# Folding packed attention values into the first expert weight: full-array fp32r products through DRAM, or fp32 products in 64x32 tiles kept on chip

## The chip, the cores and the metric

The kernel runs on one core of a Trainium2 chip. The metric is the device time of one execution in microseconds (us). The kernel before took 1387.21 us, the median of three runs (1386.0 to 1388.96). The engines of the core are called as in the profile: PE (matrix products, with PEld for its weight loads), DVE and POOL (elementwise work), ACT (activations, copies and casts), and SP, which here only issues DMAs.

## The reference

Two attentions follow one another, then a mixture of four experts that all run on every token:

```
p_packed = softmax(p k^T / 8) v            # 32 packed rows for each batch and head
out      = softmax(q p_packed^T / 8) p_packed
x        = out, heads side by side         # (8*576, 512)
y        = sum over e of  prob[:, e] * (relu(x @ w1[e]) @ w2[e])
```

There are 8 batches, 8 heads, 576 tokens per batch, head size 64; w1 is 4 x 512 x 1024 and w2 is 4 x 1024 x 512. Inputs and output are fp32.

## The kernel before

**No x is ever formed.** The second attention's weights (called xh and xl, their rounded high part and the remainder) are kept transposed: 8 heads x 32 packed rows = 256 rows, in two groups `g` of 128. Since x @ w1 = weights @ (p_packed @ w1), the kernel folds p_packed into w1 first: G = p_packed @ w1, 256 rows for each batch, formed per chunk of 512 columns of one expert's w1. There are 8 such chunks (`NCH`), two for each expert.

**Precision.** Matrix products run in fp32r, each operand split in a high part (a cast, line 86, `hi_of`) and a low part (source minus high part, line 91, `lo_of`), three products for each pair. Scores, transposes and the product with v run as plain fp32 matmuls. The profile lists each plain fp32 matmul as two records, except transposes.

**The main loop** goes over 64 units: 4 pairs of batches (`sb`), for each 8 chunks (`ch`), for each the two batches of the pair. A unit is `even` for the first batch of the pair and `odd` for the second. A unit makes:
- `mm1_group` (L316): relu(G^T x) times the probability of the expert, four groups of 12 matmuls, evicted at L322 by DVE; it runs one unit ahead.
- `s_operand` (L339 sums on DVE, then a cast on ACT and a subtraction on POOL into `st`), two products ahead.
- `product` (L395): seven Strassen-like products with combinations of w2's blocks (`tt`), 12 matmuls each; the result is added to an accumulator by DVE (L405), copied for chunk 0 (L403), finished and stored for chunk 7 (L414).

So a unit has 84 matmuls of L395 and 48 of L316, all of 288 columns. PE executes its stream in order. The order in which the code issues work is a priority; a planner that simulates times places the instructions of each engine.

**Combinations of w2** are formed in the first pair of batches only, in the odd units (`t_form`, subtractions at L377 on POOL, casts on ACT and low parts on POOL), stored to DRAM from the even units (`t_store`) and loaded again for the later pairs (`t_load`).

**G before** takes four steps. (1) `w1_split` loads a chunk of w1, splits it and writes for each head a stack of 64 rows of high part and 64 rows of low part to DRAM (`wd`); `w1_first` does this for chunk 0 without the load back. (2) `w1_loaded` loads one head's stack (`w1st`). (3) `g_heads` multiplies it with the packed values of four batches at once (`pga`, `pgb`, made by six small POOL operations at L178 to L180): two matmuls of 512 columns over the full array per head, L263 and L266, a copy by ACT to `graw` (L270), and a DMA to DRAM (`gd`) issued by ACT. (4) `g_load` loads, for each unit, the two groups of its batch (`gk`, 128 rows x 512), which are split again into `ghl`, by ACT and by DVE in the first pair of batches, by ACT and POOL after it. `g_heads` runs for batches 0 to 3 ahead of the loop and in the first pair, for batches 4 to 7 in the units from the end of the second pair through the third.

**Attention parts.** `pack_unit(b, g)` does four heads of the first attention: scores (L129), maximum, exponential, normalisation, transposes (L150, L154), product with v (L162), copy to `ppbd` (L169), and the parts for `pga` and `pgb`. `tok_unit(b, g)` does the second attention's weights for four heads: scores (L196), transposes and softmax on DVE, high and low parts. Eight pack units (batches 0 to 3) and four tok units run ahead of the loop; the other eight pack units run in the second pair of batches, the other tok units at chunks 5 to 7.

The PSUM pools are `ps_aux`, two tiles of one bank, used by transposes, the product with v and G, and `ps_dbl`, three tiles of two banks. The tiles `kt`, `vt`, `at`, `a1` of the pool `att` have one buffer each and serve pack units, tok units and `t_form` in turn.

Of the kernel before, what the change touches and what calls it, by code (L numbers as in the profile page):

```python
# [23 lines left out]
HALF = B // 2  # L24
# [15 lines left out]
def attention_moe(ctx: ExitStack, tc: tile.TileContext, q, k, v, p, dp, w1, w2, out):  # L40
# [31 lines left out]
    nc.vector.tensor_copy(  # L72
        out=pgb.rearrange("p a h n b -> p (a h n b)").rearrange("p (c n) -> p c n", c=4),
        in_=ppbd[0].rearrange("p a n -> p (a n)").rearrange("p (c n) -> p c n", c=1).broadcast_to([P, 4, NPAIR * 2 * NPK]),
    )
# [3 lines left out]
    gd = [[dram.tile([H * NPK, HALF, FC], F32, name=f"gd{hf}_{c}") for c in range(NCH)] for hf in range(2)]  # L79
    td = [[dram.tile([P, 2 * 2 * DH], F32, name=f"td{c}_{i}") for i in range(NPROD)] for c in range(NCH)]  # L80
    wd = [[dram.tile([P, FC], F32, name=f"wd{c}_{h}") for h in range(H)] for c in range(NCH)]
    pnd = dram.tile([E, NTOK], F32, name="pnd")

# [21 lines left out]
    def pack_unit(b, g, new):  # L105
        bl = b % HALF
# [18 lines left out]
        )  # L125
        sps = dbl()
# [41 lines left out]
        for hh in range(2):  # L168
            nc.vector.tensor_copy(  # L169
                out=ppbd[bl][hh * D:(hh + 1) * D, prs, hh * NPK:(hh + 1) * NPK],  # L170
                in_=psv[hh * D:(hh + 1) * D],
            )
        yield
        for hh in range(2):
            rows, other = slice(hh * D, (hh + 1) * D), slice((1 - hh) * D, (2 - hh) * D)
            src = ppbd[bl][rows, prs, hh * NPK:(hh + 1) * NPK]
            hi = pga[rows, prs, hh, :, bl]
            nc.gpsimd.tensor_copy(out=hi, in_=src)  # L178
            lo_of(pgb[rows, prs, hh, :, bl], src, hi, nc.gpsimd)
            nc.gpsimd.tensor_copy(out=pga[other, prs, hh, :, bl], in_=hi)  # L180
# [4 lines left out]
    def tok_unit(b, g):  # L185
# [3 lines left out]
        qt = att.tile([P, 2, S], F32, name="kt")  # L189
        nc.sync.dma_start(out=qt, in_=q[b][:, 2 * g:2 * g + 2, :])  # L190
        a2 = att.tile([P, S // 32, NPK], F32, name="a1")
        a2f = a2.rearrange("p a n -> p (a n)")
        ps = dbl()
        for c in range(2):
            for j in range(2):
                nc.tensor.matmul(  # L196
                    out=ps[j * 64:(j + 1) * 64, c, 0:HS], lhsT=ppbd[b % HALF][:, 2 * g + j, :],
                    rhs=qt[:, j, c * HS:(c + 1) * HS], start=True, stop=True,
                )
# [14 lines left out]
        a2t = att.tile([P, S], F32, name="at")  # L214
# [5 lines left out]
    def w1_raw(ch, pr, tile_of):  # L220
        e, hf = divmod(ch, F // FC)
        raw = tile_of()
        nc.sync.dma_start(out=raw, in_=w1[e, pr * P:(pr + 1) * P, hf * FC:(hf + 1) * FC])
        return raw

    def w1_split(ch):

        for pr in range(NPAIR):
            raw = w1_raw(ch, pr, lambda: wpool.tile([P, FC], F32, name="wraw", bufs=2))
            whl = wpool.tile([P, 2, FC], F32R, name="whl")  # L230
            hi_of(whl[:, 0, :], raw, nc.scalar)
            lo_of(whl[:, 1, :], raw, whl[:, 0, :], nc.vector)
            yield
            for hh in range(2):
                rows, other = slice(hh * D, (hh + 1) * D), slice((1 - hh) * D, (2 - hh) * D)
                dst = wd[ch][2 * pr + hh]
                nc.sync.dma_start(out=dst[rows, :], in_=whl[rows, 0, :].bitcast(F32))
                nc.sync.dma_start(out=dst[other, :], in_=whl[rows, 1, :].bitcast(F32))
            yield

    def w1_first(raws):
        for pr, raw in enumerate(raws):
            for hh in range(2):
                rows, other = slice(hh * D, (hh + 1) * D), slice((1 - hh) * D, (2 - hh) * D)
                wst = wpool.tile([P, FC], F32R, name="w1st", bufs=3)
                hi_of(wst[rows, :], raw[rows, :], nc.scalar)
                nc.vector.tensor_tensor(
                    out=wst[other, :], in0=raw[rows, :], in1=wst[rows, :].bitcast(F32), op=ALU.subtract
                )
                nc.sync.dma_start(out=wd[0][2 * pr + hh], in_=wst.bitcast(F32))  # L250
                yield wst

    def w1_loaded(ch):
        for h in range(H):
            wst = wpool.tile([P, FC], F32R, name="w1st", bufs=3)
            nc.sync.dma_start(out=wst.bitcast(F32), in_=wd[ch][h])
            yield wst

    def g_heads(half, ch, tiles):
        for h, wst in enumerate(tiles):  # L260
            yield
            ps = aux()
            nc.tensor.matmul(  # L263
                out=ps, lhsT=pga[:, h // 2, h % 2].rearrange("p n b -> p (n b)"), rhs=wst, start=True, stop=False
            )
            nc.tensor.matmul(  # L266
                out=ps, lhsT=pgb[:, h // 2, h % 2].rearrange("p n b -> p (n b)"), rhs=wst, start=False, stop=True
            )
            graw = gpool.tile([P, FC], F32, name="graw", bufs=2)
            nc.scalar.copy(out=graw, in_=ps)  # L270
            nc.scalar.dma_start(
                out=gd[half][ch][h * NPK:(h + 1) * NPK].rearrange("n b f -> (n b) f"), in_=graw
            )
            yield

    units = [(sb, ch, 2 * sb + i) for sb in range(SB) for ch in range(NCH) for i in range(2)]
    gs = {}

    def g_load(u):
        sb, ch, b = units[u]  # L280
        gs[u] = []
        for g in range(NG):
            gk = gpool.tile([P, FC], F32, name="gk", bufs=2)
            bl = b % HALF
            nc.sync.dma_start(
                out=gk,
                in_=gd[b // HALF][ch][g * P:(g + 1) * P, bl, :],
            )
            ghl = gpool.tile([P, 2, FC], F32R, name="ghl", bufs=4)
            hi_of(ghl[:, 0, :], gk, nc.scalar)  # L290
            lo_of(ghl[:, 1, :], gk, ghl[:, 0, :], nc.vector if sb == 0 else nc.gpsimd)
            gs[u].append(ghl)
            yield

# [9 lines left out]
    def mm1_group(u, kh, c):  # L304
# [4 lines left out]
        for fi in range(2):  # L309
# [3 lines left out]
            for g in range(NG):  # L313
                ghl = gs[u][g]
                for hl, rx in ((0, xl), (0, xh), (1, xh)):
                    nc.tensor.matmul(  # L316
                        out=ps[:, fi, 0:HS], lhsT=ghl[:, hl, fs], rhs=rx[:, g, ts],
                        start=n == 0, stop=n == 3 * NG - 1,
                    )
                    n += 1  # L320
# [36 lines left out]
    def t_form(ch, new):  # L357
# [15 lines left out]
        for i, name in enumerate(ORDER):  # L373
            n = of[name]
            if n in how:
                t = new([P, 2, DH], {"t1": "at", "t2": "a1", "t3": "a1", "t4": "at"}[n])
                nc.gpsimd.tensor_tensor(out=t, in0=blk[how[n][0]], in1=blk[how[n][1]], op=ALU.subtract)  # L377
# [85 lines left out]

    with ExitStack() as first:
# [6 lines left out]
        packs = [pack_unit(b, g, unit_tile(2 * b + g)) for b in range(HALF) for g in range(NG)]  # L471
        drain(wavefront(packs[:4], 1))
        raws = [w1_raw(0, pr, lambda: early.tile([P, FC], F32, name=f"w1raw{pr}")) for pr in range(NPAIR)]
        forms = t_form(0, lambda shape, name: att.tile(shape, F32, name=name))
        next(forms)
        norm_probs()
        for b in range(2):
            load_probs(b, 0)
        drain(wavefront(packs[4:], 1))
        drain(g_heads(0, 0, w1_first(raws)))  # L480
        drain(forms)
        drain(wavefront([tok_unit(0, g) for g in range(NG)], 1))
        drain(g_load(0))
        drain(w1_split(1))
        drain(wavefront([tok_unit(1, g) for g in range(NG)], 1))
        drain(g_load(1))
# [3 lines left out]

    def att_tile(shape, name):
        return att.tile(shape, F32, name=name)
# [8 lines left out]
    back, gsteps, tsteps = nothing, nothing, nothing  # L501
    GROUPS = {1: (0, 0), 3: (0, 1), 4: (1, 1), 6: (1, 0)}
    for u, (sb, ch, b) in enumerate(units):
        last_of_chunk = b % 2 == 1
        nxt = units[u + 1] if u + 1 < len(units) else None
        if not last_of_chunk:
            if ch == 0 and sb % 2 == 1 and sb + 1 < SB:
                back = chain(*[pack_unit(x, g, att_tile) for x in range(HALF, B) for g in range(NG)])
            if ch == 5 and sb + 1 < SB:
                back = chain(back, *[tok_unit(2 * sb + 2, g) for g in range(NG)])  # L510
            if ch == 7 and sb + 1 < SB and sb % 2 == 0:
                pass

        if u == 0:
            gsteps = g_heads(0, 1, w1_loaded(1))
        elif last_of_chunk:
            nsb, nch = (sb, ch + 2) if ch + 2 < NCH else (sb + 1, ch + 2 - NCH)
            gsteps = nothing
            if nsb < SB and (nsb % 2 == 0):
                if nch == 0:  # L520
                    drain(back)
                gsteps = g_heads(nsb // 2, nch, w1_loaded(nch))
# [6 lines left out]
        for i in range(NPROD):  # L529
# [16 lines left out]
            if not forming:  # L546
                next(back, None)
# [51 lines left out]
```

## Time and profile before

| what | value |
|---|---|
| median of three runs | 1387.21 us |
| the profiled execution | 1388.43 us |
| its span, first to last instruction | 1386.3 us |
| mean granted PE clock | 0.972 |
| first matmul of L395 | 101.85 us |
| PE, DVE, ACT, POOL busy | 94%, 72%, 41%, 75% |
| moved by DMA | 299.14 MB, 216 GB/s |

Durations come from one profiled execution. In lists of groups the columns are line, engine, operation, output and inputs, shapes, count, busy time in us, mean ns of one, and idle time before it with what ended it. The busy time of a group is the union of its instructions, since matmuls overlap. In tables by stretches of the span, each engine has its busy time and its count of instructions, then come the granted PE clock, the share of the DMA engines in use and the rate in GB/s.

### The profile page before, as it was taken

How to read it: one execution, taken by the hardware profiler on the slowest of the kernel's cores; microseconds unless marked ns; L12 is line 12 of the kernel's file. 1: busy time of each engine (PE TensorE's matmuls, PEld its weight loads, DVE VectorE, ACT ScalarE, POOL GpSimd, SP SyncE). 2: the span in 40 equal slices, each digit the busy share in tenths (PEclk: the TensorE clock that was granted, in tenths of full speed). 3: DMA queues.
4: the chain of work that ended last, by engine and by line, in shares of the span. 5: the costliest groups of instructions: out<-in, count | busy, mean ns of one | idle time of the engine just before them, and what ended most of it. 6: DMA issues, size and time to landing. Idle time of an engine off the chain costs nothing.

```text
span 1386.3 us, 25971 instructions
## 1 busy us (share of the span) xinstructions
PE 1303.0 (94%) x9680; PEld 1240.1 (89%) x9680; DVE 993.0 (72%) x1293; ACT 565.4 (41%) x950; POOL 1038.2 (75%) x768
## 2 busy tenths in 40 slices
PE   6669999999889999999999999999999899999997
PEld 4448998988888899999999889999999899999997
DVE  4567888989789656656766965666887946666668
ACT  3447545544332543344444444333332443333321
POOL 4619999997996767676676667777787777777775
PEclk8779999999999999999999999999999999999999
DMA  9899998998646466577887934344544644444431
GB/s 342 313 314 305 332 335 291 321 302 285 237 164 218 149 200 215 205 250 236 309 299 264 314 134 152 138 142 141 174 146 155 220 135 143 145 146 143 140 107 70
DMA packets 135069, 299.14 MB, mean 216 GB/s; under 512 B 15008, under 2 KB 33568, under 8 KB 134944
## 3 DMA queue, kind: packets, MB, share of 16 engines
q1 hardware_dynamic: 116512, 263.91, 56.8%
q10 hardware_dynamic: 18432, 33.56, 6.4%
q8 instruction: 78, 1.28, 0.4%
q14 instruction: 47, 0.39, 0.1%
HBM read 208.22 MB, written 89.20 MB: 215 GB/s over the span
## 4 chain that ended last, share of the span: by engine, by line
PE 65%; DVE 12%; POOL 9%; DMA 7%; issue 4%; ACT 2%; SPq 1%; ACTq 0%; DVEq 0%; POOLq 0%
PE dbl L395 38%; PE dbl L316 22%; DVE acc L414 4%; POOL st L91 3%; POOL tt L91 3%; DVE sblk L339 3%; DMA gd<-graw 2%; DMA wd<-whl 2%; DVE ablk L322 1%; DMA w1st<-wd 1%; PE aux L162 1%; PE aux L263 1%; POOL at L377 1%; PE aux L266 1%; DVE acc L405 1%
## 5 line engine op out<-in xcount | busy, mean ns | idle before, releaser
L395 PE MATMUL dbl<-st,tt 128*128 128x288 f32 x5376 | 777.4, 297 | 34.2 <-POOL st L91 11.9
L395 PEld LDWEIGHTS dbl<-st,tt 128*128 128x128 f32 x5376 | 739.7, 189 | 54.8 <-issue 29.2
L91 POOL TENSOR_TENSOR st<-sblk,st 128x576 fp32r<-128x576 f32 x256 | 407.0, 1597 | 197.3 <-ACT st L86 193.9
L316 PE MATMUL dbl<-xh,ghl 128*128 128x288 f32 x2048 | 419.7, 297 | 0.0
L91 POOL TENSOR_TENSOR st<-ablk,st 128x576 fp32r<-128x576 f32 x192 | 293.9, 1534 | 64.9 <-ACT st L86 63.4
L316 PEld LDWEIGHTS dbl<-xh,ghl 128*128 128x128 f32 x2048 | 332.2, 190 | 2.1
L405 DVE TENSOR_TENSOR acc<-dbl,acc 128x576 f32<-128x576 f32 x336 | 251.9, 753 | 107.9 <-PE dbl L395 107.6
L86 ACT CAST st<-sblk 128x576 fp32r<-128x576 f32 x256 | 172.9, 676 | 365.8 <-DVE sblk L339 260.5
L322 DVE SCALAR_TENSOR_TENSOR ablk<-dbl,pbt 128x576 f32<-128x576 f32 x256 | 192.5, 752 | 180.5 <-PE dbl L316 180.0
L316 PE MATMUL dbl<-xl,ghl 128*128 128x288 f32 x1024 | 305.5, 298 | 5.0 <-DVE acc L405 1.6
L86 ACT CAST st<-ablk 128x576 fp32r<-128x576 f32 x192 | 129.4, 675 | 202.7 <-PE dbl L395 178.3
L316 PEld LDWEIGHTS dbl<-xl,ghl 128*128 128x128 f32 x1024 | 194.7, 190 | 9.3 <-ACT acc L403 2.0
L91 POOL TENSOR_TENSOR ghl<-gk,ghl 128x512 fp32r<-128x512 f32 x96 | 149.8, 1579 | 0.9 <-ACT ghl L86 0.7
L339 DVE TENSOR_TENSOR sblk<-ablk 128x576 f32<-128x576 f32 x128 | 126.8, 991 | 11.6 <-DVE ablk L322 0.5
L270 ACT COPY graw<-aux 128x512 f32<-128x512 f32 x128 | 73.9, 583 | 60.7 <-PE aux L266 30.0
L86 ACT CAST ghl<-gk 128x512 fp32r<-128x512 f32 x128 | 74.8, 619 | 24.4 <-PE dbl L316 19.8
L339 DVE TENSOR_TENSOR sblk<-ablk,sblk 128x576 f32<-128x576 f32 x64 | 75.2, 1175 | 5.2
L263 PE MATMUL aux<-w1st,pga 128*128 128x512 f32 x128 | 54.0, 422 | 14.2 <-DMA w1st<-wd 5.5
L414 DVE TENSOR_TENSOR acc<-acc,acc 128x576 f32<-128x576 f32 x56 | 63.9, 1177 | 0.4
L339 DVE TENSOR_TENSOR sblk<-sblk,ablk 128x576 f32<-128x576 f32 x64 | 59.6, 930 | 1.6
L266 PE MATMUL aux<-w1st,pgb 128*128 128x512 f32 x128 | 52.4, 410 | 0.0
L403 ACT COPY acc<-dbl 128x576 f32<-128x576 f32 x56 | 35.7, 638 | 37.8 <-PE dbl L395 37.4
(71 smaller groups left out, 770.1 us busy)
## 6 DMA issues: line engine op xcount, KB each, us to landing
tt<-td SPq DMA_DIRECT2D x168, 512.0 KB, 4.6
gd<-graw ACTq DMA_DIRECT2D x128, 256.0 KB, 4.8
gk<-gd SPq DMA_DIRECT2D x128, 256.0 KB, 4.6
w1st<-wd SPq DMA_DIRECT2D x120, 256.0 KB, 5.3
td<-tt SPq DMA_DIRECT2D x56, 512.0 KB, 4.8
wd<-whl SPq DMA_DIRECT2D x112, 128.0 KB, 4.5
kt<-in_k SPq DMA_DIRECT2D x16, 576.0 KB, 5.3
kt<-in_q SPq DMA_DIRECT2D x16, 576.0 KB, 6.3
```

What stands on the lines that cost most here:

```text
L86: nc.scalar.copy(out=dst, in_=src)
L91: eng.tensor_tensor(out=dst, in0=src, in1=hi.bitcast(F32), op=ALU.subtract)
L263: nc.tensor.matmul(out=ps, lhsT=pga[:, h // 2, h % 2].rearrange("p n b -> p (n b)"), rhs=wst, start=True, stop=False)
L266: nc.tensor.matmul(out=ps, lhsT=pgb[:, h // 2, h % 2].rearrange("p n b -> p (n b)"), rhs=wst, start=False, stop=True)
L270: nc.scalar.copy(out=graw, in_=ps)
L316: nc.tensor.matmul(out=ps[:, fi, 0:HS], lhsT=ghl[:, hl, fs], rhs=rx[:, g, ts], start=n == 0, stop=n == 3 * NG - 1,)
L322: nc.vector.scalar_tensor_tensor(out=a, in0=ps[:, :, 0:HS], scalar=0.0, in1=pbt[b][:, ts].rearrange("p (o t) -> p o t", o=1).broadcast_to( ...
L339: nc.vector.tensor_tensor(out=t, in0=blk(x), in1=blk(y), op=op)
L395: nc.tensor.matmul(out=ps[:, j, 0:HS], lhsT=t[:, tl, fi, j * P:(j + 1) * P], rhs=st[:, sl, fi, :], start=n == 0, stop=n == 5,)
L403: nc.scalar.copy(out=accs[b, i], in_=psv)
L405: nc.vector.tensor_tensor(out=accs[b, i], in0=psv, in1=accs[b, i], op=ALU.add)
L414: nc.vector.tensor_tensor(out=dst, in0=x, in1=y, op=op)
```

## The change

G is formed on chip from unsplit w1 and stays there. Its core:

```diff
-    ppbd = [const.tile([P, NPAIR, 2 * NPK], F32, name=f"ppbd{i}") for i in range(HALF)]
-    pga = const.tile([P, NPAIR, 2, NPK, HALF], F32R, name="pga")
-    pgb = const.tile([P, NPAIR, 2, NPK, HALF], F32R, name="pgb")
+    ppbd = [const.tile([P, NPAIR, 2 * NPK], F32, name=f"ppbd{i}") for i in range(4)]
+    def cols(b, hh):
+        i = (hh + b) % 2
+        return slice(i * NPK, (i + 1) * NPK)
...
-    def w1_split(ch):
...
-    def w1_first(raws):
...
-    def w1_loaded(ch):
...
-    def g_heads(half, ch, tiles):
...
-    def g_load(u):
...
+    def w1_load(ch):
+        e, hf = divmod(ch, F // FC)
+        res = []
+        for pr in range(NPAIR):
+            raw = wpool.tile([P, FC], F32, name="wraw", bufs=4)
+            nc.sync.dma_start(out=raw, in_=w1[e, pr * P:(pr + 1) * P, hf * FC:(hf + 1) * FC])
+            res.append(raw)
+        return res
+    def g_form(bs, ch, raws):
+        for g in range(NG):
+            pss = {b: aux() for b in bs}
+            for hs in range(4):
+                pr, hh = 2 * g + hs // 2, hs % 2
+                rows = slice(hh * D, (hh + 1) * D)
+                for b in bs:
+                    c0 = (hs // 2) * 2 * NPK + cols(b, hh).start
+                    nc.tensor.matmul(
+                        out=pss[b][c0:c0 + NPK, :], lhsT=ppbd[b % 4][rows, pr, cols(b, hh)], rhs=raws[pr][rows, :],
+                        start=True, stop=True,
+                    )
+            for b in bs:
+                ghl = gpool.tile([P, 2, FC], F32R, name="ghl", bufs=6)
+                hi_of(ghl[:, 0, :], pss[b], nc.scalar)
+                lo_of(ghl[:, 1, :], pss[b], ghl[:, 0, :], nc.vector)
+                gs.setdefault((b, ch), []).append(ghl)
+            yield
```

One step of `g_form` (one `g`) is eight fp32 matmuls of 64 rows, 32 columns of weights and 512 columns of data: four heads for two batches. Heads alternate between rows 0 to 63 and 64 to 127 of the array. The order of the two heads of a pair within a 64-column half is swapped for odd batches, so the eight matmuls have eight different places in the array, in four column strips and two row halves, and the two batches have a PSUM bank each. In each bank both row halves write, to different partitions. The packed values are no longer split, and the low part of G is made by DVE from PSUM.

Ahead of the loop:

```diff
-        packs = [pack_unit(b, g, unit_tile(2 * b + g)) for b in range(HALF) for g in range(NG)]
...
+        packs = [pack_unit(b, g, unit_tile(2 * b + g)) for b in range(2) for g in range(NG)]
+        toks = [tok_unit(b, g, unit_tile(2 * b + g)) for b in range(2) for g in range(NG)]
+        forms = t_form(0, att_tile, nc.gpsimd)
+        for i in range(2):
+            next(packs[i])
+        raws = w1_load(0)
+        for i in range(2, 4):
+            next(packs[i])
+        norm_probs()
+        drain(wavefront(packs[:2], 1))
+        for i in range(2):
+            next(toks[i])
         next(forms)
-        norm_probs()
         for b in range(2):
             load_probs(b, 0)
...
+        drain(g_form([0], 0, raws))
+        for _ in range(2):
+            next(forms)
+        drain(wavefront(toks[:2] + packs[2:], 1))
+        for i in range(2, 4):
+            next(toks[i])
+        drain(g_form([1], 0, raws))
+        raws = w1_load(1)
+        drain(wavefront([forms] + toks[2:], 1))
```

In the loop, for every pair of batches:

```diff
+        if sb + 1 < SB:
+            nb = 2 * sb + 2
+            if not odd and 1 <= ch <= 4:
+                back = pack_unit(nb + (ch - 1) // NG, (ch - 1) % NG, att_tile)
+            elif not odd and 5 <= ch <= 6:
+                back = tok_unit(nb, ch - 5, att_tile)
+            elif ch == 7:
+                back = tok_unit(nb + 1, b % 2, att_tile)
+        gsteps = nothing
+        nsb, nch = (sb, ch + 1) if ch + 1 < NCH else (sb + 1, 0)
+        if not odd and nsb < SB:
+            gsteps = g_form([2 * nsb, 2 * nsb + 1], nch, raws)
+        tsteps = t_form(ch + 1, att_tile, nc.vector) if forming else nothing
...
+            if i in (2, 5):
                 next(gsteps, None)
...
+        if not odd:
+            nsb, nch = (sb, ch + 2) if ch + 2 < NCH else (sb + 1, ch + 2 - NCH)
+            if nsb < SB:
+                raws = w1_load(nch)
```

Four pack units so move from the part ahead of the loop into it, four for each of the first three pairs of batches. Pack and tok units issue their loads as a step of their own. w1 is loaded once for every pair of batches. The subtractions of `t_form` go to DVE for chunks 1 to 7. Apart from that, `mm1_group`, `s_operand`, `product`, `finish` and the attention's arithmetic are as before.

More of the change, by code (lines that the diff above doesn't have):

```diff
@@ L23 @@
 SB = B // 2
-HALF = B // 2
 HS = S // 2
@@ L169, in pack_unit, with tok_unit @@
             nc.vector.tensor_copy(
-                out=ppbd[bl][hh * D:(hh + 1) * D, prs, hh * NPK:(hh + 1) * NPK],
-                in_=psv[hh * D:(hh + 1) * D],
+                out=ppbd[b % 4][hh * D:(hh + 1) * D, prs, cols(b, hh)], in_=psv[hh * D:(hh + 1) * D],
             )
         yield
[L174 to L180, printed above, removed]
-        yield
     xs = {}
-    def tok_unit(b, g):
+    def tok_unit(b, g, new):
         if g == 0:
@@ L188, in tok_unit @@
         xh, xl = xs[b]
-        qt = att.tile([P, 2, S], F32, name="kt")
+        qt = new([P, 2, S], "kt")
         nc.sync.dma_start(out=qt, in_=q[b][:, 2 * g:2 * g + 2, :])
-        a2 = att.tile([P, S // 32, NPK], F32, name="a1")
+        yield
+        a2 = new([P, S // 32, NPK], "a1")
         a2f = a2.rearrange("p a n -> p (a n)")
@@ L213, in tok_unit @@
         yield
-        a2t = att.tile([P, S], F32, name="at")
+        a2t = new([P, S], "at")
         nc.vector.transpose(out=a2t, in_=a2f)
@@ L241, in w1_first @@
-    def w1_first(raws):
[L242 to L251, printed above, removed]
@@ L253, in w1_loaded @@
-    def w1_loaded(ch):
[L254 to L257, printed above, removed]
-    def g_heads(half, ch, tiles):
[L260 to L273, printed above, removed]
+            raw = wpool.tile([P, FC], F32, name="wraw", bufs=4)
@@ L313, in mm1_group @@
             for g in range(NG):
-                ghl = gs[u][g]
+                ghl = gs[b, ch][g]
                 for hl, rx in ((0, xl), (0, xh), (1, xh)):
@@ L355, in t_store, with t_form @@
         nc.sync.dma_start(out=td[ch][i], in_=tt[ch, i].rearrange("p h f d -> p (h f d)").bitcast(F32))
-    def t_form(ch, new):
+    def t_form(ch, new, eng):
         e, hf = divmod(ch, F // FC)
@@ L462, in drain, with att_tile @@
             pass
+    def att_tile(shape, name):
+        return att.tile(shape, F32, name=name)
     with ExitStack() as first:
@@ L500, in attention_moe @@
     nothing = iter(())
-    back, gsteps, tsteps = nothing, nothing, nothing
     GROUPS = {1: (0, 0), 3: (0, 1), 4: (1, 1), 6: (1, 0)}
     for u, (sb, ch, b) in enumerate(units):
-        last_of_chunk = b % 2 == 1
+        odd = b % 2 == 1
         nxt = units[u + 1] if u + 1 < len(units) else None
[L506 to L522, printed above, removed]
-        wsteps = w1_split(ch + 2) if sb == 0 and not last_of_chunk and ch + 2 < NCH else nothing
-        forming = last_of_chunk and sb == 0 and ch + 1 < NCH
-        if forming:
-            tsteps = t_form(ch + 1, att_tile)
-            next(tsteps)
-        gl = g_load(u + 2) if u + 2 < len(units) else nothing
+        back = nothing
+        if sb + 1 < SB:
[10 more added lines that the diff above has]
+            gsteps = g_form([2 * nsb, 2 * nsb + 1], nch, raws)
+        forming = odd and sb == 0 and ch + 1 < NCH
+        tsteps = t_form(ch + 1, att_tile, nc.vector) if forming else nothing
+        next(tsteps, None)
         for i in range(NPROD):
@@ L539, in attention_moe @@
                 mm1_group(u + 1, *GROUPS[i])
-            if i in (4, 6):
-                if i == 4 and u + 2 < len(units) and units[u + 2][1] % 2 == 0:
-                    load_probs(units[u + 2][2], units[u + 2][1] // 2)
-                if i == 4 and not last_of_chunk:
-                    drain(gsteps)
-                next(gl, None)
-            if not forming:
-                next(back, None)
-            if sb == 0 and not last_of_chunk:
-                t_store(ch, i)
-                next(wsteps, None)
-                if i == NPROD - 1:
-                    drain(wsteps)
-                    drain(back)
-            if last_of_chunk and nxt:
-                if forming:
-                    next(tsteps, None)
-                else:
-                    t_load(nxt[1], i)
-        if ch == NCH - 1:
-            if not last_of_chunk and sb + 1 < SB:
-                back = chain(back, *[tok_unit(2 * sb + 3, g) for g in range(NG)])
-            if last_of_chunk:
-                drain(back)
-                back = nothing
+            if i == 4 and u + 2 < len(units) and units[u + 2][1] % 2 == 0:
+                load_probs(units[u + 2][2], units[u + 2][1] // 2)
+            next(back, None)
+            next(tsteps, None)
+            if sb == 0 and not odd:
+                t_store(ch, i)
+            if odd and nxt and not forming:
+                t_load(nxt[1], i)
+        drain(back)
+        drain(gsteps)
+        if not odd:
+            nsb, nch = (sb, ch + 2) if ch + 2 < NCH else (sb + 1, ch + 2 - NCH)
+            if nsb < SB:
+                raws = w1_load(nch)
 _INS = ["q", "k", "v", "p", "dp", "w1", "w2"]
```

56 lines of the change are left out of this document (3 added, 53 removed).

## The prediction

> **What bounds the kernel now.** I read the page first, then the table by stretches, cut where the first product (L395) of each pair of batches starts.
>
> ```profile
> span 1386.3 us, 25971 instructions
> PE 1303.0 (94%) x9680; PEld 1240.1 (89%) x9680; DVE 993.0 (72%) x1293; ACT 565.4 (41%) x950; POOL 1038.2 (75%) x768
> ...
> 0.00:101.85 101.85, 67.55 (x532) 44.32 (x533) 54.22 (x121) 40.64 (x80) 42.72 (x84) 0.75 0.93 323
> 101.85:450.38 348.53, 321.26 (x2246) 306.85 (x2245) 301.31 (x325) 168.61 (x291) 318.18 (x199) 0.98 0.83 280
> 450.38:802.55 352.17, 346.47 (x2699) 327.01 (x2697) 238.01 (x332) 151.66 (x263) 241.42 (x201) 1.00 0.72 245
> 802.55:1101.38 298.83, 291.73 (x2146) 287.26 (x2145) 211.79 (x278) 106.16 (x167) 225.88 (x149) 0.98 0.45 152
> 1101.38:1379.75 278.37, 275.66 (x2065) 274.58 (x2064) 184.80 (x237) 98.31 (x153) 210.03 (x139) 1.00 0.39 129
> 1379.75:1386.30 6.55, 0.30 (x3) 0.06 (x1) 2.85 (x5) 0.00 (x0) 0.00 (x0) 0.72 0.52 180
> ```
>
> So: 101.85 us ahead of the loop, then four pairs of very unequal length, then a tail of 6.55. The next rows are an undisturbed unit, a unit with two tok units, the change of pairs from the third to the fourth (three units), the six units that hold all eight pack units of the loop, and two units of the first pair.
>
> ```profile
> 878.97:896.53 17.56, 17.56 (x134) 17.56 (x133) 11.21 (x15) 5.87 (x10) 13.42 (x10) 1.00 0.18 59
> 984.33:1004.52 20.19, 20.19 (x150) 18.59 (x149) 18.80 (x27) 7.04 (x11) 16.27 (x11) 1.00 0.40 125
> ...
> 1057.20:1121.43 64.23, 58.16 (x415) 55.36 (x413) 57.19 (x70) 22.90 (x37) 46.10 (x29) 0.97 0.44 145
> ...
> 450.38:591.95 141.57, 139.09 (x1234) 128.98 (x1233) 87.51 (x140) 59.82 (x112) 100.93 (x109) 1.00 0.58 195
> ...
> 145.13:186.95 41.82, 39.74 (x284) 38.36 (x283) 37.41 (x39) 22.95 (x41) 40.42 (x25) 1.00 0.97 346
> ```
>
> A clean unit is PE alone: 17.56 of 17.56 us busy, at full clock. Whatever PE is given in the last three pairs is paid in full, and whatever leaves the other engines there is worth nothing. In the first pair POOL (40.42 of 41.82) and DMA (0.97) are as full as PE. One head of `g_heads` costs PE two steps of 0.23:
>
> ```profile
> 116.51 0.23 PE aux L263
> 116.74 0.23 PE aux L266
> ```
>
> From this I build the loop before, in us. 64 units are 64 x 17.56 = 1123.8. A tok unit is (20.19 - 17.56) / 2 = 1.32; twelve are 15.8. A change of pairs is 64.23 - 3 x 17.56 - 2 x 1.32 = 8.9; three are 26.7. A pack unit, with eight heads (3.8) also in that stretch, is (141.57 - 6 x 17.56 - 3.8) / 8 = 4.05; eight are 32.4. 120 heads in the loop are 120 x 0.47 = 56.4. The last two units are 5.1 short of full, since the measure ends with the last product's start. The sum is 1250.0, and the loop took 1379.75 - 101.85 = 1277.9: the 27.9 left is stall, which I put into the first pair.
>
> **The change, part by part. PE's new work** decides. No row shows a 64x32 tile; the nearest are the scores of a tok unit, four fp32 matmuls (eight records) of 288 columns in two column strips, inside the unit above.
>
> ```profile
> 986.02 0.46 PE L196 MATMUL dbl<-kt,ppbd 128*64 128x288 f32 x2
> ...
> 986.02 1.19 PE L196 MATMUL dbl<-kt,ppbd 128*64 128x288 f32 x8
> ```
>
> The first row is what runs in a window of 0.1 us near the start: two records at once, in the same 0.46. All eight take 1.19, so each further pair adds (1.19 - 0.46) / 3 = 0.243: two strips run side by side at the price of one. The block costs PE 1.32, so 1.32 - 4 x 0.243 = 0.34 is entry and exit. For 512 columns a slot is 0.243 x 512 / 288 = 0.432. A step of `g_form` has eight matmuls, 16 records. If all eight places run together it is 2 x 0.432 + 0.34 = 1.21, and I take 1.25 for the starts of six more; if two at a time, as far as the rows go, 8 x 0.432 + 0.34 = 3.80; four at a time, 2.07. I take 1.25: the rows show concurrency that is complete, not partial, and all eight places differ. There are 31 x 2 = 62 steps in the loop: 77.5, where the heads were 56.4. PE's work for G grows.
>
> "TensorE: Matmul & The Clock Gate" of the Trainium skill (Part 3, Measured speedup) gives 10.6 times for sixteen matmuls packed by rows and columns. By it the step stays near 1.2; no run here shows it yet. Against the change speaks "TensorEngine Tiling (Array Packing)" of the Trainium skill (Restrictions and Gotchas, Gotcha 1): different row tiles cannot access the same PSUM bank simultaneously. Here both row halves write each bank; by that rule the step is the 3.80 of the first rival, and this trace, which has tiles that start at row 0 alone, shows neither.
>
> **Moved pack units.** Twelve instead of eight in the loop: 12 x 4.05 = 48.6, so +16.2. Their loads stand ahead of `t_store` and `w1_load` on SP and wait there for `kt` and `vt`, which `t_form` holds to the end of the odd unit; what queues behind them is due a unit later, and the pack's scores come one product (about 2.5 us) after the issue. If the load lands after that, the planner's order of PE stalls. The 4.05 already holds such waits; 6 each at worst.
>
> **Ahead of the loop.** What goes is the round trip of G:
>
> ```profile
> 67.97 4.08 DMA gd<-graw
> 72.74 7.35 DMA gd<-graw
> 80.78 6.50 DMA gd<-graw
> 88.67 5.32 DMA gd<-graw
> 94.07 4.74 DMA gd<-graw
> ...
> 24.47 0.47 DVE L169 COPY ppbd<-aux 64x64 f32<-64x64 f32 x2 [2.17 <-PE aux L162]
> ...
> 63.35 2.05 PE L196 MATMUL dbl<-kt,ppbd 128*64 128x288 f32 x8
> ...
> 74.95 1.40 POOL L91 TENSOR_TENSOR xl<-at,xh 128x576 fp32r<-128x576 f32 x1 [7.95 <-ACT xh L86]
> ...
> 92.46 0.61 PE L316 MATMUL dbl<-xl,ghl 128*128 128x288 f32 x1
> ...
> 101.85 1.35 PE L395 MATMUL dbl<-st,tt 128*128 128x288 f32 x9
> ```
>
> The five rows of the chain are 28.0 us of waiting for that buffer's DMA. Forward for the new start: batch 0 is packed at 24.9, as now. Its q follows k and v of two batches and one chunk of w1, about 7 MB, at the 323 GB/s of the first stretch 21.5 us; tok starts at 25, with G's two steps beside it. A tok unit takes 63.35 to 76.35, so 13.0; the second shares DVE, +5: 43. From first L316 to first L395 now 9.4: 52.4. Batch 1's pack and tok units and its G stand ahead in DVE's priority; +4 gives 56 (47 if they fit in the gaps, 70 if all goes first). That gains 46.
>
> **First pair.** The rows, first four subtractions of `t_form` in the chunk shown above, then DVE's and POOL's low parts, ACT's copy, and the DMAs that go:
>
> ```profile
> 145.13:186.95 41.82, 6.60 (x4) 1.00 0.97 346
> ...
> 78.64 0.69 DVE L91 TENSOR_TENSOR ghl<-gk,ghl 128x512 fp32r<-128x512 f32 x1 [3.96 <-ACT ghl L86]
> L91 DVE TENSOR_TENSOR whl<-wraw,whl 128x512 fp32r<-128x512 f32 x28 | 31.9, 1140 | 3.3 <-ACT whl L86 3.3
> L91 POOL TENSOR_TENSOR ghl<-gk,ghl 128x512 fp32r<-128x512 f32 x96 | 149.8, 1579 | 0.9 <-ACT ghl L86 0.7
> L270 ACT COPY graw<-aux 128x512 f32<-128x512 f32 x128 | 73.9, 583 | 60.7 <-PE aux L266 30.0 <-DMA gd<-graw 28.4 <-PE dbl L316 2.0
> gd<-graw ACTq DMA_DIRECT2D x128, 256.0 KB, 4.8
> gk<-gd SPq DMA_DIRECT2D x128, 256.0 KB, 4.6
> w1st<-wd SPq DMA_DIRECT2D x120, 256.0 KB, 5.3
> ```
>
> POOL has 40.42 - 6.60 = 33.8 per chunk, against PE's 2 x 17.56 + 2 x 1.25 + 4.05 = 41.7. DVE had 37.41; it gains the four subtractions (about 1.1 each by the row of `whl`, 4.4), loses four of `whl` (4.6), and a pack unit's 2.6 comes: about 40, no longer far from PE. DMA loses the last three rows (376 transfers of 256 KB, 98 MB of the page's 299 over the whole span) and gets three more readings of w1, 25 MB; its 0.97 is no bound any more. So two of the three causes of the 27.9 go and one grows: I take 9 of it (0 to 27.9).
>
> **Edits at nothing.** ACT loses 128 copies (73.9) and DMA issues; it bounds nothing. Later pairs: 96 low parts leave POOL (149.8) and come to DVE at about 0.69, two per unit, under 17.56 - 11.21 of idle DVE; at a change of pairs, where DVE had 57.19 of 64.23, four of them (2.8) have less cover, but one of the two tok units of the odd unit (5.1 on DVE) moves to the even one. I leave 8.9. The load of w1 is issued a unit ahead; if it were late, each chunk would lose up to its landing of about 5.
>
> **Sum.** Loop: 1123.8 + 15.8 + 26.7 + 48.6 + 77.5 - 5.1 + 9 = 1296.3. Start 56, tail 6.55: span 1358.9. The profiled execution took 1388.43, 2.1 over its span: 1361.0, against 1388.43 now. The median of the runs, 1387.21, is 1.2 lower: **1360 us**, 2.0% faster. The change is paid by the start (-46) and given back in part by the loop (+18).
>
> **The rivals.**
> - *Tiles two at a time* (the row halves take turns at a bank, or PE's order holds later tiles back): 62 x (3.80 - 1.25) = 158, and four steps at the start of 0.86 more: 1521. For it: no row shows more than two. Against: those two are complete. The change breaks even at 27 / 62 + 1.25 = 1.69 per step. Chance 0.13. Four at a time, 1360 + 62 x 0.82 = 1411: 0.10.
> - *A wait for the aux banks.* A step takes both PSUM tiles that pack units also use; the next transposes wait for two casts (0.6) and two subtractions (0.69), 2.6. Paid at each of twelve pack units it is +31: 1391, slower; it decides from 2.3 each. For it: pack's second step falls on the same product as a step of G. Against: the planner moves PE's work around. 0.14.
> - *Better*: start 47 and no stall in the first pair: 1360 - 18 = 1342. For it: POOL and DMA both fall clear of the bound. Against: DVE rises. 0.13.
> - *The forecast*, 1345 to 1378: 0.50.
>
> **How the numbers follow.** Below 1335 I leave 0.05, above 1420 the 0.13 of the first rival and a little more; the four-at-a-time case is inside. Range 1335 to 1420. A measurement of this kernel tells about 0.2% (2.8 us) from no change. Faster: 0.50 + 0.13 + 0.04 of the aux case = 0.67; same 0.05 of it; slower 0.13 + 0.10 + 0.05 = 0.28.
>
> **What would show it.** The new matmul group: eight matmuls in about 1 us and a loop unit with two steps at 20.1 confirm 1.25; 25 refutes it. The first L395 near 56. In the first pair POOL near 80% and PE over 95%. PE idle after `g_form` released by DVE would be the aux rival. A clean unit other than 17.56, or a start past 75, would make the forecast wrong.

## The result, and the profile after

The changed kernel takes **1434.60 us** (median of four runs, 1433.95 to 1435.22); the kernel before, run beside it, takes 1388.09 (four runs, 1386.0 to 1389.18). The ratio is 1.0337, with a 95% interval of 1.0319 to 1.0355: slower by 3.4%. The prediction, 1360 with a range of 1335 to 1420, was wrong in sign and range.

| us | forecast | measured | difference |
|---|---|---|---|
| start, to the first product | 56 | 71.76 | +15.8 |
| loop | 1296.3 | 1354.25 | +58.0 |
| tail | 6.55 | 6.59 | 0.0 |
| span | 1358.9 | 1432.6 | +73.7 |

The page of the changed kernel, its head and the groups that answer to those of before. Line numbers have moved: L340 is the product (L395 before), L261 `mm1_group`, L228 the matmul of `g_form`, L82 and L87 the high and low parts.

```profile
span 1432.6 us, 26109 instructions
PE 1382.6 (97%) x10448; PEld 1205.5 (84%) x10448; DVE 999.7 (70%) x1380; ACT 477.0 (33%) x786; POOL 795.8 (56%) x548
DMA packets 84631, 208.94 MB, mean 146 GB/s; under 512 B 8608, under 2 KB 27168, under 8 KB 84512
L228 PE MATMUL aux<-wraw,ppbd 64*32 64x512 f32 x1024 | 149.2, 612 | 0.0
L87 DVE TENSOR_TENSOR ghl<-aux,ghl 128x512 fp32r<-128x512 f32 x128 | 85.6, 684 | 41.8 <-ACT ghl L82 41.3
```

Everything that the change was to relieve is relieved: POOL falls from 75% to 56%, ACT from 41% to 33%, DMA from 299 to 209 MB. PE alone rises, from 1303.0 us to 1382.6, with 768 more records. The matmuls of `g_form` are busy for 149.2 us, and PE was never idle ahead of one. Next the table by stretches, cut as before at the first product of each pair of batches, and then three units of the last pair, which holds no pack or tok units.

```profile
0.00:71.76 71.76, 45.06 (x349) 27.08 (x349) 44.54 (x85) 22.13 (x43) 29.69 (x34) 0.83 0.75 251
71.76:430.63 358.87, 352.11 (x2624) 300.93 (x2621) 283.44 (x359) 135.97 (x229) 248.46 (x168) 1.00 0.46 156
430.63:776.93 346.30, 341.91 (x2614) 299.42 (x2613) 237.05 (x337) 111.21 (x182) 175.31 (x120) 1.00 0.45 144
776.93:1123.27 346.34, 341.96 (x2615) 299.46 (x2613) 237.08 (x337) 111.20 (x182) 174.07 (x116) 1.00 0.44 141
1123.27:1426.01 302.74, 301.24 (x2257) 278.56 (x2256) 194.70 (x262) 96.51 (x151) 168.30 (x111) 1.00 0.36 115
...
1142.90:1165.01 22.11, 22.11 (x144) 18.11 (x143) 8.13 (x12) 9.38 (x16) 11.04 (x8) 1.00 0.53 166
1165.01:1188.41 23.40, 23.40 (x153) 18.39 (x153) 12.83 (x17) 5.91 (x9) 10.22 (x8) 1.00 0.14 48
...
1210.77:1229.53 18.76, 18.76 (x151) 17.76 (x149) 12.16 (x17) 5.81 (x10) 10.21 (x8) 1.00 0.16 54
```

PE is busy for every microsecond of these units, at full clock, yet they take 22.11, 23.40 and 18.76. A clean unit before took 17.56. The chain of the same kernel shows why; its columns are start, duration, engine and tile, line, and the records that ran in a row. First the 22.11 us unit, then the 18.76 us one:

```profile
1143.06 3.20 PE dbl L340 x24
1146.26 1.58 PE dbl L261 x12
1147.84 0.97 PE aux L228 x2
1148.81 3.38 PE dbl L340 x24
1152.19 1.60 PE dbl L261 x12
1153.79 0.97 PE aux L228 x2
1154.77 1.80 PE dbl L340 x12
1156.57 1.59 PE dbl L261 x12
1158.16 0.98 PE aux L228 x4
1159.14 3.39 PE dbl L340 x24
1162.53 1.58 PE dbl L261 x12
1164.11 0.97 PE aux L228 x2
...
1214.13 1.58 PE dbl L261 x12
1215.71 1.02 PE aux L228 x16
1216.73 3.38 PE dbl L340 x24
```

In the second unit a whole step, 16 records, is one stretch of 1.02 us, and the work behind it takes 0.18 longer than elsewhere (3.38 against 3.20): 18.76 - 17.56 = 1.20, the step as forecast. In the first unit four stretches hold two, two, four and two records, ten in all, and each takes 0.97 or 0.98, with the same 0.18 or so behind it. That unit pays (22.11 - 17.56) / 4 = 1.14 for each; the delay behind the fourth falls into the next unit. **One matmul (two records) costs PE almost what eight matmuls cost.** In the whole trace the 66 steps of `g_form`, four of them ahead of the loop, run as 138 separate stretches, counted as runs of L228 records with another line's before and behind. 132 of them stand behind the first product, so in the loop as it is measured here; one and a half of the loop's steps run ahead of it.

The code issues the eight matmuls of a step in one go. It is the planner, which places each instruction by its simulated times, that put products and `mm1_group` between them.

The start is late for another reason. In the same kernel, the stretches of the start behind batch 0's packing, and rows of the chain through them:

```profile
30.00:45.00 15.00, 2.59 (x13) 1.75 (x10) 14.76 (x25) 7.94 (x17) 13.61 (x14) 0.62 0.94 331
45.00:57.00 12.00, 11.52 (x116) 6.46 (x114) 4.11 (x10) 1.91 (x4) 4.04 (x3) 0.62 0.73 234
57.00:71.76 14.76, 10.39 (x75) 7.80 (x73) 14.36 (x23) 5.28 (x9) 5.61 (x4) 0.88 0.34 114
```

```profile
31.09 6.82 DMA pt<-in_p
...
46.86 6.66 DMA vt<-in_w
...
53.54 0.69 DVE a L322
...
54.26 0.22 DVE ppbd L165
...
64.34 1.62 DVE a L200
...
66.69 0.73 DVE ablk L267
...
67.46 2.95 PE dbl L261 x12
70.41 1.42 PE aux L228 x8
71.83 0.33 PE dbl L340
```

DVE is full in the first and the third stretch (14.76 of 15, 14.36 of 14.76), so batch 1's softmax (L200 and what is around it) delays batch 0's first eviction (L267) to 66.69. Between them, `t_form`'s subtraction (L322) waited on DVE for its transfer to 53.54, with batch 1's packed copies (L165) behind it.

PE came late as well. These two rows are from the timelines of POOL and PE in the same kernel: the last operand part of batch 0 (`xl`), and the first matmul of `mm1_group`.

```profile
47.64 1.40 POOL L87 TENSOR_TENSOR xl<-at,xh 128x576 fp32r<-128x576 f32 x1
...
56.98 0.40 PE L261 MATMUL dbl<-xl,ghl 128*128 128x288 f32 x1
```

Batch 0's weights were complete at 49.04. PE reached them at 56.98, since batch 1's product with v, its G and its scores stood ahead in PE's order.

### The profile page after: what moved, and what is told of

The parts are those of the page before. It is cut to its first block, busy times and chain, and to the rows that moved or that the text cites. A ratio compares the mean times of both kernels' runs of the same rounds, so it can differ in the third digit from the quotient of the medians.

```text
span 1432.6 us, 26109 instructions
## 1 busy us (share of the span) xinstructions
PE 1382.6 (97%) x10448; PEld 1205.5 (84%) x10448; DVE 999.7 (70%) x1380; ACT 477.0 (33%) x786; POOL 795.8 (56%) x548
## 4 chain that ended last, share of the span: by engine, by line
PE 84%; DVE 9%; DMA 3%; issue 2%; POOL 1%; SPq 0%; ACT 0%; DVEq 0%; ACTq 0%; POOLq 0%
PE dbl L340 46%; PE dbl L261 26%; PE aux L228 9%; DVE acc L359 4%; DVE sblk L284 2%; PE aux L158 1%; DVE ablk L267 1%; DMA vt<-in_v 1%; DMA kt<-in_w 1%; PE dbl L125 1%; PE dbl L184 1%; DMA pt<-in_p 0%; DMA vt<-in_w 0%; DVE a L193 0%; POOL tt L87 0%
## 5 line engine op out<-in xcount | busy, mean ns | idle before, releaser
L340 PEld LDWEIGHTS dbl<-st,tt 128*128 128x128 f32 x5376 | 728.9, 188 | 85.0 <-issue 48.2
L340 PE MATMUL dbl<-st,tt 128*128 128x288 f32 x5376 | 778.4, 297 | 14.3 <-DVE acc L359 6.3
L87 POOL TENSOR_TENSOR st<-sblk,st 128x576 fp32r<-128x576 f32 x256 | 392.9, 1540 | 311.6 <-ACT st L82 308.2
L87 POOL TENSOR_TENSOR st<-ablk,st 128x576 fp32r<-128x576 f32 x192 | 286.5, 1494 | 242.1 <-ACT st L82 218.9
L261 PE MATMUL dbl<-xh,ghl 128*128 128x288 f32 x2048 | 418.7, 295 | 0.0
L261 PEld LDWEIGHTS dbl<-xh,ghl 128*128 128x128 f32 x2048 | 329.5, 188 | 10.1 <-issue 10.1
L267 DVE SCALAR_TENSOR_TENSOR ablk<-dbl,pbt 128x576 f32<-128x576 f32 x256 | 192.9, 754 | 205.2 <-PE dbl L261 203.7
L261 PE MATMUL dbl<-xl,ghl 128*128 128x288 f32 x1024 | 307.7, 301 | 7.1 <-DVE ablk L267 5.2
L82 ACT CAST st<-sblk 128x576 fp32r<-128x576 f32 x256 | 172.9, 675 | 343.7 <-DVE sblk L284 209.5
L261 PEld LDWEIGHTS dbl<-xl,ghl 128*128 128x128 f32 x1024 | 192.4, 188 | 45.3 <-DVE acc L350 29.3
L82 ACT CAST st<-ablk 128x576 fp32r<-128x576 f32 x192 | 129.6, 675 | 253.9 <-PE dbl L340 240.3
L228 PE MATMUL aux<-wraw,ppbd 64*32 64x512 f32 x1024 | 149.2, 612 | 0.0
L284 DVE TENSOR_TENSOR sblk<-ablk 128x576 f32<-128x576 f32 x128 | 116.0, 906 | 8.7
L87 DVE TENSOR_TENSOR ghl<-aux,ghl 128x512 fp32r<-128x512 f32 x128 | 85.6, 684 | 41.8 <-ACT ghl L82 41.3
L82 ACT CAST ghl<-aux 128x512 fp32r<-128x512 f32 x128 | 72.4, 589 | 98.2 <-PE aux L228 80.3
L284 DVE TENSOR_TENSOR sblk<-ablk,sblk 128x576 f32<-128x576 f32 x64 | 54.8, 857 | 3.3
L228 PEld LDWEIGHTS aux<-wraw,ppbd 64*32 64x32 f32 x1024 | 21.4, 105 | 24.3 <-issue 21.1
L87 POOL TENSOR_TENSOR xl<-at,xh 128x576 fp32r<-128x576 f32 x16 | 26.8, 1676 | 22.8 <-ACT xh L82 22.8
```

The lines of the kernel that those rows point to most:

```text
L82: nc.scalar.copy(out=dst, in_=src)
L87: eng.tensor_tensor(out=dst, in0=src, in1=hi.bitcast(F32), op=ALU.subtract)
L228: nc.tensor.matmul(out=pss[b][c0:c0 + NPK, :], lhsT=ppbd[b % 4][rows, pr, cols(b, hh)], rhs=raws[pr][rows, :], start=True, stop=True,)
L261: nc.tensor.matmul(out=ps[:, fi, 0:HS], lhsT=ghl[:, hl, fs], rhs=rx[:, g, ts], start=n == 0, stop=n == 3 * NG - 1,)
L267: nc.vector.scalar_tensor_tensor(out=a, in0=ps[:, :, 0:HS], scalar=0.0, in1=pbt[b][:, ts].rearrange("p (o t) -> p o t", o=1).broadcast_to( ...
L284: nc.vector.tensor_tensor(out=t, in0=blk(x), in1=blk(y), op=op)
```

## The experiments

**The theory:** a stretch of `g_form` in PE's order costs about 1.17 us whatever it holds, and the loop pays for 132 of them instead of 62. **The rivals:** the tiles do not all run side by side; or a step waits for its two PSUM banks. For the start: batch 1's work ahead of the loop, by way of DVE, against batch 0's own loads.

### One step, one stretch

Seven matmuls of a step are tied behind its first, at highest priority, to keep the planner from putting anything between them; the first is that of the bank allocated second.

```diff
+            first = None
...
-                for b in bs:
+                for b in bs[::-1]:
...
+                    with ExitStack() as held:
+                        if first is not None:
+                            held.enter_context(tc.high_priority())
+                            held.enter_context(tc.issue_after(first.ins))
+                        mm = nc.tensor.matmul(
...
+                    first = first or mm
```

> Same work as the changed kernel; the eight matmuls of a step are tied behind its first one and given the highest priority, so that PE's order has them in 81 separate pieces instead of 138. Theory (a piece costs PE about 1.06 to 1.20 us whatever it holds, since it runs two slots of 0.43 us and pays entry and exit): 57 pieces fewer, 57 x 1.06 to 1.20 = 60 to 68 us less, 1366 to 1375 us, faster than the kernel before. Rival 1 (the cost goes with the number of matmuls, the pieces only fill time in which PE would have waited): no change, 1430 to 1436 us. Rival 2 (the changed kernel is slow by the moved pack units and by waits on DVE): also within 10 us of 1434.6.

Measured: 1373.13 us (1372.29 to 1374.75), ratio to before 0.9888, interval 0.9872 to 0.9903. Nothing of the arithmetic differs from the changed kernel, and it is 61 us faster. The trace has 81 stretches, 75 in the loop, and the loop takes 1291.64. 29 of the 75 hold half a step, four matmuls. The second variant takes the step's PSUM from one two-bank tile of `ps_dbl`, so that it never waits for two banks one after the other:

```diff
-            pss = {b: aux() for b in bs}
+            pd2 = dbl()
+            pss = {b: pd2[:, i, :] for i, b in enumerate(bs)}
```

> As the run before, but a step takes one of the three two-bank PSUM tiles in place of the two single banks, so that nothing but its own tile holds it: 66 pieces, the least but two. Theory: 72 pieces fewer than in the changed kernel, 76 to 86 us less, 1348 to 1358 us, unless the products wait for the tile taken from them (up to 62 x 1.4 us of eviction by ACT and DVE if nothing covers it). Rivals: 1430 to 1436 us.

Measured: 1386.34 us, ratio 0.9974 (0.9957 to 0.9991), 28 to 38 over what was expected. There are 66 stretches, one for each step, so that aim was met; new waits took a good part of the gain. PE's waits in the loop of this run (what waited, for whom: us, times, longest):

```profile
PE dbl L347 <- DVE acc L357: 12.3, 13, 3.2
PE dbl L347 <- DVE acc L366: 8.3, 9, 1.3
PE dbl L347 <- POOL st L87: 7.3, 7, 2.5
```

Products (L347 here) wait 20.6 us that DVE's evictions end: `g_form` now takes one of the three two-bank tiles that these empty. In the changed kernel all its waits for DVE in the loop were some 12 us. PE's whole idle time in the loop is 34.8 us here and 17.0 in the changed kernel, so 17.8 of the excess is idle time, and 3.6 is a later start (75.36); the rest I did not take apart. The two spare single banks were the cheaper place.

### More stretches on purpose, and an earlier place

The third variant goes the other way: the changed kernel with each step cut into four by hand, a pair of matmuls behind each product, as far as there are products: 203 of its stretches in the loop hold one pair, 15 hold three.

```diff
+                        if behind:
+                            held.enter_context(tc.high_priority())
+                            held.enter_context(tc.issue_after(behind[-1].ins))
...
+                if behind and hs < 3:
+                    yield
...
-            if i in (2, 5):
+            next(gsteps, None)
+            if i == 3:
                 next(gsteps, None)
```

> Same work as the changed kernel, the other way: each pair of matmuls of a step is tied behind a different product, 222 pieces instead of 138. Theory: 84 pieces more, 84 x 1.06 to 1.20 = 89 to 101 us more, 1520 to 1540 us. Rival 1 (cost by matmuls): 1430 to 1440 us. Rival 2: 1430 to 1440 us.

Measured: 1534.53 us in one run, with 222 stretches. In its last pair two units side by side, the first without a step, the second with eight stretches of four records:

```profile
1211.69:1229.25 17.56, 17.56 (x134) 17.56 (x133) 6.79 (x9) 8.56 (x15) 10.10 (x8) 1.00 0.57 191
1229.25:1256.17 26.92, 26.92 (x167) 18.89 (x165) 13.21 (x18) 6.86 (x11) 11.29 (x8) 1.00 0.20 65
```

(26.92 - 17.56) / 8 = 1.17. PE is busy throughout: no wait is in it. Two more runs keep the code of a step and move its place to behind the first and second product, ahead of the pack unit's transposes:

```diff
-            if i in (2, 5):
+            if i in (0, 1):
                 next(gsteps, None)
```

Once on top of the tied steps (and of the return of four subtractions to POOL, below), once on the changed kernel as it was.

> This is e5_sub_pool with the two steps of g_form entered behind the first and the second product of the even unit, ahead of the pack unit's transposes, instead of behind the third and the sixth. PE's order then holds 69 stretches of g_form in place of 81, and only four of those in the loop are halves of a step. If a stretch costs PE 1.17 us whatever it holds, the loop loses 12 x 1.17 = 14 us against e5_sub_pool: 1357 to 1360 us. If what cost was not the number of stretches but that the steps stand between a pack unit's parts and wait for their banks, or if w1's chunk lands too late for the earlier place, the loop stays at 1285 or more and the time at 1366 to 1376.

> This is the changed kernel with the same earlier place for the two steps and nothing that ties a step's matmuls together. PE's order then holds 152 stretches of g_form in place of 138. If the number of stretches is the price, the time rises by 14 x 1.17 = 16 us over the changed kernel: 1446 to 1455 us. If the place is what matters, it falls towards 1420.

Measured: **1356.67 us** (1355.85 to 1357.04) for the tied one, ratio to before 0.9780, interval 0.9756 to 0.9803: the fastest of all, 2.2% under the kernel before. The loose one took 1450.11 in one run. The same edit gains 15 us in one and costs 15 in the other; what goes with the time is the count of stretches.

| kernel | stretches in the loop | loop, us | of it PE idle | line through the ends |
|---|---|---|---|---|
| tied, early | 63 | 1274.5 | 16.7 | 1274.5 |
| tied | 75 | 1291.6 | 19.0 | 1288.4 |
| the changed kernel | 132 | 1354.3 | 17.0 | 1354.6 |
| loose, early | 146 | 1369.7 | 15.9 | 1370.9 |
| cut by hand | 218 | 1454.5 | 14.2 | 1454.5 |

The last column is 1274.5 + (n - 63) x (1454.5 - 1274.5) / (218 - 63), that is 1.161 us for each stretch. The three kernels between lie within 3.2 us of the line through the two ends, and PE's idle time does not grow with the time, so it is not waiting that tells the five apart. The variant with the two-bank tile does not lie on the line: with 62 stretches its loop takes 1304.1, 31 above it. The count sets the loop only where the steps add no waits.

### Four places for eight matmuls

This undoes the swap of the two heads for odd batches, on the variant with the two-bank tile: eight matmuls now have four places.

```diff
-        i = (hh + b) % 2
+        i = hh
```

> As the run with whole steps in a two-bank tile, but the order of two heads is not swapped for odd batches: the two batches then want the same four places of the array, so that eight matmuls have four places instead of eight. Theory (only different places run side by side; a slot of 512 columns is 0.43 us): a step goes from 1.20 to 1.20 + 2 x 0.43 = 2.06, 62 steps in the loop and none of the four single-batch steps change: 53 us more than that run. Rival (places do not matter once matmuls stand together): the same time as that run.

Measured: 1420.0 us in one run, 33.7 over the variant with the swap. A unit with two steps, in the table by stretches, without the swap:

```profile
1145.86:1167.56 21.70, 21.70 (x167) 18.57 (x166) 13.85 (x19) 6.87 (x11) 10.84 (x8) 1.00 0.28 86
```

and the same unit with it:

```profile
1124.24:1144.22 19.98, 19.98 (x167) 17.97 (x165) 13.85 (x19) 6.87 (x11) 10.85 (x8) 1.00 0.30 93
```

A step costs (21.70 - 17.56) / 2 = 2.07 with four places and (19.98 - 17.56) / 2 = 1.21 with eight. The prediction had worked out 2.07 and 1.21. So all eight places do run side by side. The time rose by less than 62 x 0.86 = 53, in part because PE was waiting in the variant with the swap: its idle time in the loop falls from 34.8 to 20.1 us, 14.7 of the missing 20. The rest I did not take apart.

### The start

All four are edits of the tied variant. First, batch 1's pack and tok units ahead of the loop are left out (the first pair then uses batch 0's weights for batch 1, and its G for chunk 0, so the output is not the reference's):

```diff
-        for i in range(2, 4):
-            next(packs[i])
...
-        drain(wavefront(toks[:2] + packs[2:], 1))
-        for i in range(2, 4):
-            next(toks[i])
-        drain(g_form([1], 0, raws))
+        drain(wavefront(toks[:2], 1))
+        xs[1], gs[1, 0] = xs[0], gs[0, 0]
...
-        drain(wavefront([forms] + toks[2:], 1))
+        drain(forms)
```

> The run with whole steps in single banks, without the work for batch 1 ahead of the loop: its pack units, tok units and G of chunk 0 are left out, and the loop uses batch 0's weights and G of chunk 0 in their place (the output for batch 1 is then not the reference's). The forecast put the start for batch 0 alone at 52.4 us and the work for batch 1 at 4 more. Theory: batch 0 alone is near 52 and batch 1 costs 20, since DVE and PE work through it first: first product at 50 to 55, whole 1350 to 1356 us. Rival (the start is long for batch 0 itself, by loads and by POOL's combinations of w2): first product above 62.

Measured: 1349.32 us in one run. The start of it, and of the tied variant:

```profile
0.00:50.82 50.82, 31.37 (x234) 17.78 (x235) 27.93 (x53) 15.98 (x30) 23.00 (x30) 0.90 0.84 295
```

```profile
0.00:72.11 72.11, 45.48 (x348) 26.82 (x349) 44.47 (x85) 21.87 (x43) 29.31 (x34) 0.74 0.74 250
```

Batch 0 alone is ready at 50.82, where the forecast had 52.4. Batch 1 costs 21.3 us more, of which the forecast had 4. DVE loses 44.47 - 27.93 = 16.5 us of work, PE 14.1. Batch 1's loads go too, so this run shows what batch 1 costs but not by which engine.

Then the subtractions of `t_form` for chunk 1, which stood on DVE waiting for a transfer, back on POOL:

```diff
-        tsteps = t_form(ch + 1, att_tile, nc.vector) if forming else nothing
+        tsteps = t_form(ch + 1, att_tile, nc.vector if ch else nc.gpsimd) if forming else nothing
```

> The run with whole steps in single banks (1373.13 us, first product at 72.11), with one edit: the four subtractions of w2's blocks for chunk 1 go back to POOL; those of chunks 2 to 7 stay on DVE. Theory: in the changed kernel one of them waits on DVE for its load from 49.2 to 53.5 us and holds back the copy of batch 1's packed values, which PE had ready at 51.4; without it the first product starts 2 to 3 us earlier, near 69 to 70, and the whole takes 1370 to 1371 us. Rival (DVE has slack there, or POOL's added work ahead of the low parts of x costs as much): first product within 1 us of 72, 1373 us.

Measured: 1371.97 us, ratio 0.9875 (0.9853 to 0.9897), not to be told from the tied variant; the start came at 71.14, 1.0 earlier, where two to three were expected. That wait was in the chain, and when it left, little else moved. Next, the first unit's `mm1_group` and operands at highest priority, alone and with the edit above:

```diff
+    with tc.high_priority():
+        for kh, c in ((0, 0), (0, 1), (1, 1), (1, 0)):
+            mm1_group(0, kh, c)
+        for i in range(LA):
+            s_operand(0, i)
```

> The run with whole steps in single banks, with one edit: the first unit's four groups of matmuls, their evictions and its first two operands get the highest priority in the planner, ahead of batch 1's second attention, where the code had them behind it. Theory (the order on DVE behind batch 1 holds the first product back, as the first eviction at 66.7 us comes right after batch 1's last softmax operation): the first product starts 8 to 14 us earlier, at 58 to 64; the whole gains less, since batch 1 is then due in the first unit: 2 to 8 us, 1365 to 1371. Rival (x of batch 0 itself comes late, at 49.0 us, and PE is busy with batch 1's pack units until 57): within 3 us of 72, 1372 to 1374 us.

> Both edits of the two runs before together, on the run with whole steps in single banks. If they act on the same stretch one after another, the gains add: 3 us and what the priority gives, 1362 to 1370 us. If one hides the other, the better of the two alone.

Measured: 1376.70 us (ratio 0.9904, 0.9884 to 0.9923) and 1377.26 (0.9903, 0.9883 to 0.9923), both slower than the tied variant. The first product does come earlier, at 68.09 in the first of them, but by 4.0 and not by the 8 to 14 expected: PE came to its first `mm1_group` at 57.27, where the tied variant came at 58.64. And the first unit then takes 27.9 us instead of 20.05: the tok unit that was pushed back is needed there. The chain of that run:

```profile
74.23 4.72 POOL st L87 x3
78.96 1.37 POOL xl L87
...
80.37 2.53 PE dbl L267 x9
```

PE's next `mm1_group` (L267) stands until 80.37 for batch 1's `xl`, behind three operand parts on POOL. Batch 1's work was not surplus that a priority could remove: in both runs the first unit lost more than the start gained.

## Why the prediction was wrong, by its own steps

**The step that failed: "There are 31 x 2 = 62 steps in the loop: 77.5".** The number of steps is right and so is the price of one; what PE pays for is not steps but entries into the 64x32 tiling, and the loop makes 132 of them. The forecast's own formula, two slots and 0.34 of entry and exit, gives the same 1.20 for one matmul as for eight, since one matmul is two records one behind the other in one place. I applied it only to whole steps. That a planner orders PE's stream stood in the kernel's description, and the aux rival even leaned on "the planner moves PE's work around"; I took that as cover and not as a price. By the line of the table, 62 stretches would give a loop of 1273.3, and 70 more at 1.161 are 81.3: 1354.6.

**What hid part of it.** The loop's other terms were too dear by 1296.3 - 1273.3 = 23.0, so the loop missed by 58 and not by 81. Two stretches of the fastest variant, a chunk with one pack unit and two whole steps, and a unit with one tok unit and one step:

```profile
443.26:484.47 41.21, 41.21 (x352) 38.09 (x350) 27.71 (x41) 13.05 (x23) 20.72 (x15) 1.00 0.49 159
...
608.09:627.98 19.89, 19.89 (x159) 18.26 (x157) 16.52 (x26) 6.39 (x11) 11.44 (x8) 1.00 0.27 97
```

A pack unit is 41.21 - 2 x 17.56 - 2 x 1.20 = 3.69, not 4.05, and a tok unit 19.89 - 18.76 = 1.13, not 1.32: 4.3 and 2.3 over twelve of each. The step at 1.20 for 1.25 gives 3.1. The first pair of batches takes 331.80 there against 325.94 for the second, so by that comparison the stall that I put at 9 is 5.9. The tok unit is cheaper for a reason: its scores, a tiled stretch too, stand right behind the step there, and the 0.18 behind a stretch is paid once for both. These are 12.8 of the 23.0. The three changes of pairs, three units each, take 194.71 there; less nine clean units, nine steps and six tok units that is 6.4 for each, not 8.9, which gives 7.6 more. The rest I did not take apart.

**The start: "+4 gives 56".** Batch 0's 52.4 held (50.8). Batch 1 came at 21.3, which puts the start past the 70 that the forecast named for the case that all of it goes first. I saw that DVE was shared and priced it as if gaps were there; the table has DVE full in two of three stretches, and PE's order, which the forecast did not price there, kept batch 0 waiting from 49.04 to 56.98. Against 101.85 before, the start still gained 30.

**The rivals.** *Tiles two or four at a time* did not come: a whole step takes 1.20, and four places take the 2.07 worked out for them. Here both row halves write each bank within one stretch of 1.02 us. Turns at a bank would have made the step the 3.80 of the first rival, or, with the two banks at work side by side, the 2.07 of four places. By the Trainium skill's "TensorEngine Tiling (Array Packing)" (Restrictions and Gotchas, Gotcha 1) different row tiles cannot access the same bank simultaneously; the trace disagrees. *A wait for the aux banks* did not show as a wait: PE is idle for 0.0 us ahead of L228. The two banks may still be what leaves 29 half steps in the tied variant: with both in one tile no step of the loop was halved. *Better*, 1342, fell with the start and the loop. No rival held the mechanism that decided.

**What was right:** PE as the bound and the clean unit of 17.56, the step's price, eight places at once, the relief of POOL and of the DMA (share 0.46 in the first pair, from 0.83), the low part of G at 0.68 us on DVE. With the steps tied together in the two single banks, the loop came out 5 and 22 us under the forecast (1291.6 and 1274.5 against 1296.3). That the fastest variant's 1356.67 is near the 1360 of the forecast is luck: its loop is 22 shorter than forecast and its start, at 73.07, is 17 later, and the two misses cancel.

That the count of stretches sets the loop, where no waits are added, is shown by five kernels. Why the planner took the steps apart is not: tying them undoes it, and an earlier place alone makes it worse.

## What to carry to other kernels

Before pricing small work on the engine that is the bound, ask how often that engine will enter it, and count the entries in the instruction order instead of the calls in the code: here a short tiled matmul cost its entry, and its neighbours in other places of the tiling were nearly free. Where a planner orders the engine, tie such a group together, take its PSUM from where nobody else on the path waits, and check that the group is still whole in the trace. When work moves ahead of a loop, add up each engine's busy time in that window before calling any of it hidden.

## What the runs showed of the hardware

Stretches of fp32 matmuls in 64x32 tiles between products over the full array held PE for 0.97 to 0.98 us with one or two matmuls and 1.02 us with eight, and the first products behind took about 0.18 longer. In four places, two matmuls each, the stretch was 1.87 us:

```profile
1152.40 1.87 PE dbl L234 x16
1154.27 1.80 PE dbl L347 x12
```

A second matmul in each place so adds about 0.85 us, and the eight places hardly slow one another, though two row halves write to one bank: 1.02 us with eight against 0.97 with one.
